# Loading w_down weights a pair ahead, and moving row and z loads, in an FNet/GeGLU kernel

## The chip, the cores and the metric

The kernel runs on one core of a Trainium2 chip. The metric is the device time of one execution in microseconds (us); the time before is the median of three runs. Beside them one execution was recorded by the hardware profiler, and everything that is read from the profile comes from that one.

The engines, as the profile names them: PE (TensorE, matmuls; PEld are its weight loads), DVE (VectorE), ACT (ScalarE), POOL (GpSimd) and SP (SyncE, which here only issues DMAs). DMAs are issued by SP and by POOL.

## What is computed

Four layers over x of 2048 rows and 512 columns, in single precision: a Fourier mixing layer and a gated feed-forward layer, twice.

```python
def _A_ref(x, dft_seq_re, dft_seq_im, dft_hid_re, dft_hid_im):
    a = jnp.einsum("bsd,ed->bse", x, dft_hid_re)
    b = jnp.einsum("bsd,ed->bse", x, dft_hid_im)
    y = jnp.einsum("ts,bse->bte", dft_seq_re, a) - jnp.einsum("ts,bse->bte", dft_seq_im, b)
    return y

def _B_ref(x, w_gate, w_up, w_down):      # w_gate, w_up: 512 x 1792, w_down: 1792 x 512
    return (_gelu(x @ w_gate) * (x @ w_up)) @ w_down

x = x + _A_ref(_layernorm(x, axis=-1), dft_seq_re, dft_seq_im, dft_hid_re, dft_hid_im)
x = x + _B_ref(_layernorm(x, axis=-1), w_gate, w_up, w_down)
x = x + _A_ref(_layernorm(x, axis=-1), dft_seq_re, dft_seq_im, dft_hid_re, dft_hid_im)
x = x + _B_ref(_layernorm(x, axis=-1), w_gate, w_up, w_down)
```

## The kernel before

**Products.** Every single precision operand is split in two parts, `hi` (ACT, line 150) and `lo` (DVE, line 152), and a product is three matmuls (`mm3`, lines 207 to 209). The kernel multiplies 2x2 blocks of matrices with seven products instead of eight, in Winograd's form: A11, A12, S1 to S4, A22 are the blocks and sums of blocks of one operand, B11 to B22 and T1 to T4 those of the other. The sums S1 to S4 of a weight are made once on DVE (`sums` in `weight_steps`, four operations of 256 columns), split (`divide`), kept in DRAM by POOL's DMAs and loaded from there afterwards: `wb` for w_gate and w_up, `wc` (the DRAM tiles `wdd`) for w_down.

**Layers.** `mix` does layers 0 and 2, `geglu(w, layer)` one half (w = 0 or 1: 1024 rows) of layers 1 and 3. In `geglu` the loop runs `up(n)` for 14 n; each n is one block column of w_gate or w_up and has seven products of six matmuls, and beside them one product of the down projection (`beside`, `down_product`), so 8 x 6 = 48 matmuls in most n. What is left of the down projection follows as the late part: 36 products of six (25 in the second half of layer 3, which ends with `plain_rows`). `down_order` gives their order.

**Queues and lists of small work.** The order of the work is written by hand. `queue` holds small pieces of work; each `step()` (one at each product of `up`, one at each product of the late part) takes one. `slow` is a second such list, of which every `PACE`-th step takes one. `chores` and `down_making` are two more. The framework then orders each engine's instructions by its own model of time; instructions of one engine run in that order. `issue_after` puts an instruction behind a given one on the same engine's queue.

**Operand stream.** `take()` hands out the next operand of PE and calls loads ahead of it (`load_next`, line 328, on SP): `wc` pieces two products ahead in `up`, six ahead in the late part. `stream["last"]` is the load that was called last.

**Slots.** SBUF has 98 slots of 128 x 512 (`sb`). They are handed out from a list in which a slot that comes free goes to the end; a load into a slot waits for the slot's last user.

The parts that the change touches:

- `down_piece`, `load_next` and `divide`: how a pair of w_down's blocks lies in DRAM. A tile `wdd[k]` holds three pairs of pieces of 1024 columns and one single. In a pair, the `hi` parts of both pieces come first and then the `lo` parts, so one piece is two rows of 256 columns (1 KB) in each partition.
- `down_making`: the making of w_down's seven pieces pairs k. For each k there are six entries, the load (three DMAs, lines 956 to 958, source `wdc`), `sums` and four `divide`. `DOWN_RUNS` says how many entries are taken where: 24 in layer 0, and 2 at each `up(n)` with n > 2 in the first half of layer 1.
- `terms_ahead` (line 573): mean and deviation of the rows of x for layer 2. It is called from `slow` in the second half of layer 1, eight times; each loads a row block (line 235, SP), and has three ACT passes (lines 565 to 570) and two small POOL operations.
- `block_steps(layer, 1)`: the second half's normed input z, transposed through DRAM (`turned`, tile `t`). `others[:ND]` are four `fetch` (line 687, eight DMAs of 64 KB each on SP for w = 1), the rest are differences and splits on DVE and ACT.
- `load_turned` (line 1249, DMAs of line 1253 on SP): loads the rows of x to which the down projection is added, in wide tiles, `xwide` for part 0 and `wide` for part 1, four DMAs of 256 KB each, in runs of 128 columns. It is called for part 0 at the last product beside `up`, where all seven pairs are used a second time after the loop, and for part 1 when the late part is a third through. Sums are added into these tiles by DVE in `turned_rows`.

Of the kernel before, what the change touches and what calls it, by code (L numbers as in the profile page):

```python
# [17 lines left out]
ND = D // P  # L18
# [15 lines left out]
PACE = 9  # L34
# [5 lines left out]
LEAD = 3  # L40
NK = NS // 2
SEED_AT = 3
DOWN_RUNS = ((0,0,0,0),(4,4,4,0),(4,4,4,0),2)


@with_exitstack
def fnet_geglu(ctx: ExitStack, tc: tile.TileContext, x_in, ws, wh, wgu, wdn, wdc, out):
# [32 lines left out]
    nc = tc.nc  # L80
# [56 lines left out]
    def f32(ap):  # L137
        return ap.bitcast(F32)
# [72 lines left out]
    half = slice(0, 256), slice(256, 512)  # L211
# [84 lines left out]
    wdd = {k: dram.tile([P, 7 * 512], F32, name=f"wc{k}") for k in range(NF // 2)}  # L296
    pieces = (("A11", "A12"), ("S2", "S3"), ("S1", "A22"), ("S4",))

    def down_piece(k, name):

        i = next(i for i, names in enumerate(pieces) if name in names)
        if i == 3:
            return wdd[k][:, 3 * 1024:]
        h = half[pieces[i].index(name)]
        return wdd[k][:, i * 1024:(i + 1) * 1024].rearrange("p (h c) -> p h c", h=2)[:, :, h]

    def halves(t):
        return t[:, :512], t[:, 512:]
# [1 line left out]
    def kept(place, parts):  # L310
        for t, a in zip(parts, halves(place)):
            nc.gpsimd.dma_start(a, f32(t))  # L312
# [3 lines left out]
    stream = {"loaded": 0, "split": 0, "used": 0, "more": 0}  # L316
    raws, parts = {}, {}

    def load_next():
        n = stream["loaded"]  # L320
        dtype, addresses, _, _ = items[n]
        raws[n] = []
        for a in addresses:
            t = sb.get(dtype)
            to = t if dtype == F32 else f32(t)
            if len(a.shape) == 3:
                to = to.rearrange("p (h c) -> p h c", h=2)
            stream["last"] = nc.sync.dma_start(to, a)
            raws[n].append(t)
        stream["loaded"] += 1  # L330
# [117 lines left out]
    NP = NF // 2  # L448
# [62 lines left out]
                items.extend((F32, (wdn[f],), plain, None) for f in range(2 * SEVEN[layer + 1, w], NF))  # L511


    queue, slow, steps_done, down_making = [], [], [0], []

    def step():
        if queue:
            run = queue.pop(0)
            if run is not None:
                run()  # L520
        steps_done[0] += 1
        if slow and steps_done[0] % PACE == 0:
            slow.pop(0)()


# [47 lines left out]
    def terms_ahead(layer, i, n):  # L573

        if i == 0:
            fresh["terms"] = x_load(layer, 0)
        x, junk = fresh.pop("terms"), sb.get()
        if i + 1 < n:
            fresh["terms"] = x_load(layer, i + 1)
        known[layer, i] = norm_terms(layer, i, x, junk)  # L580
        sb.put(x, junk)
# [156 lines left out]
    def mix(layer):  # L738
# [65 lines left out]
        def a11(b):  # L804
            chain = [ps8.get() for _ in range(2)]
            for k in range(NK):
# [6 lines left out]
                else:  # L813
                    six(chain, "B11", k, k == 0, k == NK - 1, "11" if b == NB - 1 else None)
                if b == FORE[layer] - 1 and k == SEED_AT:
                    a12_seeded(0)
# [104 lines left out]
        for n, (b, what) in enumerate(plan(layer)):  # L921
            if n == len(plan(layer)) - 1:
                if layer:
                    weight_load(0)
                    weight_load(1)
                while queue:
                    step()
            in_order[0] = layer or (b, what) not in plan(layer)[:2 * FORE[layer]]
            if layer == 0 and (b, what) == (0, "S2"):
                for k in range(NP):  # L930
                    load, making = down_weight_steps(k)
                    down_making.extend([load] + making)
            if what in stages:
                stages[what](b)
            else:
                hid_groups(b, what)
# [5 lines left out]
    wblocks = {n: dram.tile([P, 7 * 512], F32, name=f"wb{n}") for n in range(NF)}  # L942
# [3 lines left out]
    def weight_steps(n, raw=wgu, place=wblocks):  # L946

        src, v = [], {}

        def load():  # L950
            src.extend(sb.get() for _ in range(4))
            for i, names in enumerate((*pieces[:3], ("S4", "A21"))):
                for name, h in zip(names, half):
                    v[name] = src[i][:, h]
            with tc.issue_after(stream["last"].ins):
                nc.sync.dma_start(src[0], raw[n, :, :512])
                nc.sync.dma_start(v["A22"], raw[n, :, 512:768])
                nc.sync.dma_start(v["A21"], raw[n, :, 768:])

        def sums():  # L960
            before, in_order[0] = in_order[0], True
            plus(v["S1"], v["A21"], v["A22"])
            minus(v["S2"], v["S1"], v["A11"])
            minus(v["S3"], v["A11"], v["A21"])
            minus(v["S4"], v["A12"], v["S2"])
            in_order[0] = before

        def divide(i):
            def run():
                before, in_order[0] = in_order[0], True  # L970
                to = place[n][:, i * 1024:min((i + 1) * 1024, 7 * 512)]
                if i < 3:
                    t = split_slot(src[i])
                    kept(to, t)
                else:
                    t = (split_side(v["S4"]),)
                    nc.gpsimd.dma_start(to, f32(t[0]))
                if place is wblocks:
                    piece_here(n, i, t)
                else:  # L980
                    sb.put(*t)
                sb.put(src[i])
                in_order[0] = before
            return run

        return load, [sums] + [divide(i) for i in range(len(pieces))]

    def down_weight_steps(k):
        return weight_steps(k, wdc, wdd)
# [27 lines left out]
    def geglu(w, layer):  # L1017

        gs, h, acc = {}, {}, {0: [], 1: []}
# [31 lines left out]
        making = {}  # L1051
# [191 lines left out]
        def rows_moved(at, part, run):  # L1243

            for p in range(NT):
                v = xturned[part][p * 32:(p + 1) * 32]
                run(v.rearrange("t (j e) -> t j e", e=P), turned_view(at, part)[p])

        def load_turned(part):
            assert part or not sb.out("x")  # L1250
            pool = tpool if part else upool
            xturned[part] = pool.tile([P, NT * D], F32, name="wide" if part else "xwide")
            rows_moved(layer, part, lambda v, outside: nc.sync.dma_start(v, outside))

        def turned_rows(part, c, src):

# [58 lines left out]
        before_mix = w == 1 and layer < 3  # L1315
        plain_down = (layer, w) not in SEVEN
        if before_mix:
            slow.extend((lambda k=k: terms_ahead(layer + 1, k, NK)) for k in range(NK))
        if w == 0:
            norms, others = block_steps(layer, 1)  # L1320
            slow.extend(norms)
            ahead_of_all = others[:ND]
        if not plain_down and layer == 1 or layer == 3:
            sb.reclaim("x")
        first(0)
# [14 lines left out]
        elif pairs == NP:  # L1340
            load_turned(0)
        if w == 0:
            queue.extend(([None] * 4 if ahead_of_all else []) + others[len(ahead_of_all):])
        elif before_mix:
            queue.extend((lambda k=k: first_rows(layer + 1, k)) for k in range(NK))
        ahead = [(lambda n=n, i=i: piece_load(n, i)) for n in range(2) for i in range(len(pieces))]
# [154 lines left out]
```

## Time and profile before

| | us |
|---|---|
| median of 3 runs | 1626.48 |
| lowest and highest of them | 1619.25, 1629.77 |
| the profiled execution | 1617.86 |
| its span, first to last instruction | 1615.7 |
| mean granted PE clock in the span | 0.998 |

A line of the page's list of groups, here the first of the three matmuls of a product, and the two lines of the splits:

```profile
L207 PE MATMUL p<-s,s 128*128 128x512 f32 x2320 | 870.9, 391 | 10.7 <-DMA s<-wc 4.2
L150 ACT ACTIVATE s<-s 128x512 fp32r<-128x512 f32 (+1 forms) x809 | 454.9, 607 | 264.0 <-DVE s L183 72.9
L152 DVE TENSOR_TENSOR s<-s,s 128x512 fp32r<-128x512 f32 (+1 forms) x809 | 510.8, 669 | 121.0 <-ACT s L150 102.4
```

To be read as: line, engine, operation, output and inputs by the program's names (numbers of buffers left out; `s` are the slots, `p` the banks of PSUM), shape, count; then the group's busy time in us and the mean of one in ns; then the engine's idle time just before instructions of this group, and what ended most of it. The matmuls overlap in the pipeline, so that the mean of one is longer than the distance between two.

In timelines a row has its start and its length in us, the engine, line and operation, and in brackets how long the engine stood idle before it and what ended that. In the list of DMA issues, the last column is the median time from issue to landing.

### The profile page before, as it was taken

The numbers are of one execution on the slowest core, as the hardware profiler recorded it, in microseconds if no ns is written. First come the engines' busy times: TensorE is split into PE (matmuls) and PEld (weight loads), VectorE is DVE, ScalarE is ACT, GpSimd is POOL, SyncE is SP. The second block draws the span as 40 slices with busy tenths as digits, with TensorE's granted clock in tenths as the row PEclk, the third lists the DMA queues.
The fourth block names the chain that finished last, engine by engine and source line by source line (L and its number), as shares of the span: only waits on it lengthen the run. The fifth ranks groups of instructions, "written<-read, shape, count | busy, mean of one in ns | idle before, by whom it ended". The sixth has DMA issues, their size and how long they took to land. (4 is left out here: it accounts for less than half of the span.)

```text
span 1615.7 us, 22644 instructions
## 1 busy us (share of the span) xinstructions
PE 1598.9 (99%) x7008; PEld 1317.2 (82%) x7008; DVE 1133.3 (70%) x1958; ACT 885.4 (55%) x1711; POOL 260.9 (16%) x469
## 2 busy tenths in 40 slices
PE   9999999999999999999999999999999999999998
PEld 7888888888788878788788888888888888888887
DVE  8997778797689784445879967777764457743574
ACT  8955466664667552645648545565555455433460
POOL 4112121242456101100031000101400000000001
PEclk9999999999999999999999999999999999999999
DMA  9878887996988899954986866878989676895445
GB/s 359 292 266 305 284 312 263 339 327 214 335 307 320 271 309 304 248 168 138 319 285 201 269 238 224 283 246 283 267 282 301 191 222 189 309 302 175 125 150 156
DMA packets 258840, 419.14 MB, mean 259 GB/s; under 512 B 28512, under 2 KB 106592, under 8 KB 257696
## 3 DMA queue, kind: packets, MB, share of 16 engines
q1 hardware_dynamic: 234480, 336.16, 65.2%
q0 software_dynamic: 24240, 81.55, 14.2%
q8 instruction: 55, 0.90, 0.2%
q14 instruction: 65, 0.53, 0.1%
HBM read 341.31 MB, written 76.28 MB: 258 GB/s over the span
## 5 line engine op out<-in xcount | busy, mean ns | idle before, releaser
L208 PE MATMUL p<-s,s 128*128 128x512 f32 x2320 | 902.6, 390 | 0.0
L209 PE MATMUL p<-s,s 128*128 128x512 f32 x2320 | 895.8, 390 | 0.0
L207 PE MATMUL p<-s,s 128*128 128x512 f32 x2320 | 870.9, 391 | 10.7 <-DMA s<-wc 4.2
L150 ACT ACTIVATE s<-s 128x512 fp32r<-128x512 f32 (+1 forms) x809 | 454.9, 607 | 264.0 <-DVE s L183 72.9
L152 DVE TENSOR_TENSOR s<-s,s 128x512 fp32r<-128x512 f32 (+1 forms) x809 | 510.8, 669 | 121.0 <-ACT s L150 102.4
L207 PEld LDWEIGHTS p<-s,s 128*128 128x128 f32 x2320 | 436.2, 188 | 104.8 <-DMA s<-wc 5.5
L208 PEld LDWEIGHTS p<-s,s 128*128 128x128 f32 x2320 | 436.6, 188 | 91.0 <-DVE s L152 0.7
L209 PEld LDWEIGHTS p<-s,s 128*128 128x128 f32 x2320 | 436.5, 188 | 90.4
L187 DVE TENSOR_TENSOR s<-s,p 128x512 f32<-128x512 f32 x188 | 127.5, 685 | 175.6 <-PE p L209 146.5
L183 DVE TENSOR_TENSOR s<-s,s 128x512 f32<-128x512 f32 (+1 forms) x374 | 224.8, 619 | 7.9 <-PE p L208 3.7
L194 ACT ACTIVATE s<-p 128x512 f32<-128x512 f32 x232 | 134.0, 594 | 112.0 <-PE p L209 107.6
L1014 ACT ACTIVATE s<-s 128x512 f32<-128x512 f32 x84 | 52.7, 629 | 69.1 <-DVE s L187 66.9
L568 POOL TENSOR_SCALAR rstd<-rstd 128x1 f32<-128x1 f32 x40 | 22.3, 556 | 347.4 <-ACT s L567 331.9
L152 DVE TENSOR_TENSOR s<-xwide,s 128x512 fp32r<-128x512 f32 x71 | 48.3, 687 | 33.9 <-ACT s L150 33.6
L1028 DVE TENSOR_TENSOR s<-s,p 128x512 f32<-128x512 f32 x56 | 38.4, 686 | 31.5 <-PE p L209 28.2
L312 POOL DMA_DIRECT2D wb<-s x84 | 45.8, 548 | 90.1 <-ACT s L150 61.5
L190 DVE TENSOR_TENSOR s<-s,s 128x512 f32<-128x512 f32 (+1 forms) x68 | 41.1, 613 | 16.5 <-DMA s<-wdc 9.8
L150 ACT ACTIVATE s<-xwide 128x512 fp32r<-128x512 f32 x71 | 43.1, 621 | 17.2 <-DVE xwide L183 6.6
L591 ACT ACTIVATE s<-s,shift,rstd 128x512 f32<-128x512 f32 x56 | 45.0, 811 | 11.3 <-DMA s<-x 5.7
L201 ACT ACTIVATE p<-p 128x512 f32<-128x512 f32 x56 | 32.7, 585 | 27.9 <-PE p L209 27.7
L1014 ACT ACTIVATE s<-p 128x512 f32<-128x512 f32 x28 | 16.7, 598 | 52.8 <-PE p L209 49.1
L565 ACT ACTIVATE s<-s 128x512 f32<-128x512 f32 x33 | 20.7, 627 | 42.1 <-DMA s<-x 22.2
(100 smaller groups left out, 601.5 us busy)
## 6 DMA issues: line engine op xcount, KB each, us to landing
s<-ws SPq DMA_DIRECT2D x384, 256.0 KB, 4.9
s<-wb SPq DMA_DIRECT2D x294, 256.0 KB, 4.9
s<-wc SPq DMA_DIRECT2D x182, 256.0 KB, 4.7
s<-wh SPq DMA_DIRECT2D x116, 256.0 KB, 5.1
wb<-s POOLq DMA_DIRECT2D x98, 256.0 KB, 4.7
s<-x SPq DMA_DIRECT2D x59, 256.0 KB, 5.2
xwide<-ws SPq DMA_DIRECT2D x50, 256.0 KB, 4.8
wc<-s POOLq DMA_DIRECT2D x49, 256.0 KB, 6.0
```

The source lines that it names most:

```text
L150: newest["ACT"] = nc.scalar.activation(hi, src, AF.Copy)
L152: newest["DVE"] = nc.vector.tensor_tensor(lo, src, f32(hi), op=ALU.subtract)
L183: nc.vector.tensor_tensor(out, a, b, op=ALU.subtract)
L187: bank_read["DVE"] = nc.vector.tensor_tensor(out, a, b, op=ALU.add)
L190: nc.vector.tensor_tensor(out, a, b, op=ALU.add)
L194: bank_read["ACT"] = nc.scalar.activation(v, src, AF.Copy)
L207: nc.tensor.matmul(ps, ah, bh, start=start, stop=False, skip_group_check=True)
L208: nc.tensor.matmul(ps, ah, bl, start=False, stop=False, skip_group_check=True)
L209: nc.tensor.matmul(ps, al, bh, start=False, stop=stop, skip_group_check=True)
L312: nc.gpsimd.dma_start(a, f32(t))
L591: nc.scalar.activation(z, x, AF.Identity, bias=shift, scale=rstd)
L1014: nc.scalar.activation(t, g, AF.Gelu_apprx_tanh)
```

## The change

Four things change.

1. w_down in DRAM: within a pair of pieces the `hi` and `lo` of one piece now lie together, so a piece is read as one row of 512 columns (2 KB) in each partition, and a `divide` of w_down writes two rows of 256 columns (1 KB) for each of its two tiles.
2. `down_making`: up to k = `MIXED` = 4 the load of pair k stands before its own sums as now; with k = 4 also the load of pair 5 is called before the sums of pair 4, and then always the next pair's load before this pair's sums.
3. In the second half of layer 1, `slow` gets four empty entries ahead of the eight `terms_ahead`, and its pace is 7 steps instead of 9 (back to 9 at the next first half). In the first half of layer 1 the four fetches of z no longer run at `up(13)` but in the late part, behind four empty entries, and four more empty entries follow them. Layer 3 keeps its order.
4. `load_turned` in second halves (w = 1): its DMAs are put behind the operand load that was called last before it.

```diff
+MIXED = 4
...
-        h = half[pieces[i].index(name)]
-        return wdd[k][:, i * 1024:(i + 1) * 1024].rearrange("p (h c) -> p h c", h=2)[:, :, h]
+        at = i * 1024 + pieces[i].index(name) * 512
+        return wdd[k][:, at:at + 512]
...
-            if len(a.shape) == 3:
-                to = to.rearrange("p (h c) -> p h c", h=2)
...
-    queue, slow, steps_done, down_making = [], [], [0], []
+    queue, slow, steps_done, pace, down_making = [], [], [0], [PACE], []
...
-        if slow and steps_done[0] % PACE == 0:
+        if slow and steps_done[0] % pace[0] == 0:
             slow.pop(0)()
...
+                runs = [down_weight_steps(k) for k in range(NP)]
                 for k in range(NP):
-                    load, making = down_weight_steps(k)
-                    down_making.extend([load] + making)
+                    loads = [runs[k][0]] * (k <= MIXED) + [load for load, _ in runs[k + 1:k + 2] if k >= MIXED]
+                    down_making.extend([*loads, *runs[k][1]])
...
                     t = split_slot(src[i])
-                    kept(to, t)
+                    if place is wblocks:
+                        kept(to, t)
+                    else:
+                        for a, h in zip(t, range(2)):
+                            at = to.rearrange("p (n h c) -> p h n c", n=2, h=2)[:, h]
+                            nc.gpsimd.dma_start(at, f32(a).rearrange("p (n c) -> p n c", n=2))
...
-            rows_moved(layer, part, lambda v, outside: nc.sync.dma_start(v, outside))
+            with tc.issue_after(stream["last"].ins) if w else ExitStack():
+                rows_moved(layer, part, lambda v, outside: nc.sync.dma_start(v, outside))
...
         if before_mix:
-            slow.extend((lambda k=k: terms_ahead(layer + 1, k, NK)) for k in range(NK))
+            slow.extend([lambda: None] * 4 + [(lambda k=k: terms_ahead(layer + 1, k, NK)) for k in range(NK)])
+            pace[0] = 7
         if w == 0:
+            pace[0] = PACE
             norms, others = block_steps(layer, 1)
             slow.extend(norms)
-            ahead_of_all = others[:ND]
+            ahead_of_all = others[:ND] if layer in (3,) else []
...
         if w == 0:
-            queue.extend(([None] * 4 if ahead_of_all else []) + others[len(ahead_of_all):])
+            queue.extend([None] * 4 + others[len(ahead_of_all):ND] + ([] if ahead_of_all else [None] * 4) + others[ND:])
```

## The prediction

> **What bounds the kernel now.** I read the page first, for the engines' shares.
>
> ```profile
> span 1615.7 us, 22644 instructions
> PE 1598.9 (99%) x7008; PEld 1317.2 (82%) x7008; DVE 1133.3 (70%) x1958; ACT 885.4 (55%) x1711; POOL 260.9 (16%) x469
> ```
>
> TensorE (PE) has work 99% of the span, so only its few stops can be won. To price them I cut the span at the starts of the program's stages. Matmuls start in program order, so a stage's first one is found by counting: one `up(n)` is 8 products of 6 matmuls, a late part 36 products of 6. The view of busy time by windows then gives each stage's length (the first column behind the edges; the x counts take in one or two matmuls at the edges):
>
> ```profile
> core 0: us, PE busy (x) PEld busy (x) DVE busy (x) ACT busy (x) POOL busy (x), PEclk, DMA share, GB/s
> 424.27:435.15 10.88, 10.88 (x50) 9.02 (x48) 6.13 (x11) 7.99 (x17) 5.10 (x10) 1.00 1.07 341
> 435.15:451.48 16.33, 12.75 (x49) 10.12 (x48) 10.10 (x22) 6.22 (x12) 5.70 (x11) 0.90 0.88 323
> 557.62:609.36 51.74, 49.53 (x217) 40.44 (x216) 44.89 (x74) 27.43 (x49) 0.00 (x0) 1.00 0.90 300
> 643.36:658.64 15.28, 12.86 (x50) 9.70 (x48) 4.37 (x7) 12.95 (x39) 4.13 (x10) 0.89 1.11 286
> 764.72:815.62 50.90, 49.39 (x218) 40.41 (x217) 43.96 (x76) 32.75 (x61) 0.00 (x0) 1.00 0.86 286
> 1358.36:1408.24 49.88, 49.26 (x217) 40.50 (x216) 43.45 (x72) 26.86 (x48) 0.00 (x0) 1.00 0.91 308
> 1589.12:1615.72 26.60, 21.92 (x97) 17.85 (x95) 9.20 (x14) 0.00 (x0) 5.88 (x11) 1.00 0.78 237
> ```
>
> The first row is `up(2)` of layer 1, first half, undisturbed: 48 matmuls in 10.88 us, 0.2267 us each. A late part of 216 would take 48.96. What each stage loses is its length less that:
> - layer 1, first half (w=0), `up(3)`: 16.33 - 10.88 = 5.45; its late part: 51.74 - 48.96 = 2.78
> - layer 1, second half (w=1), `up(3)`: 15.28 - 10.88 = 4.40; its late part: 50.90 - 48.96 = 1.94
> - layer 3, first half, late part: 49.88 - 48.96 = 0.92
>
> Together 15.5 us. The last row, the 96 matmuls of `plain_rows`, loses 26.60 - 21.76 = 4.84 to the closing adds and stores, which the change leaves alone. PE's timeline shows one stop in each of the five stages and, in brackets, who ended it:
>
> ```profile
> 441.61 0.80 PE L207 MATMUL p<-s,s 128*128 128x512 f32 x1 [3.58 <-DVE s L1028]
> 572.96 0.50 PE L207 MATMUL p<-s,s 128*128 128x512 f32 x1 [2.09 <-DMA s<-wc]
> 649.79 1.22 PE L207 MATMUL p<-s,s 128*128 128x512 f32 x2 [2.18 <-ACT s L150]
> 779.65 0.50 PE L207 MATMUL p<-s,s 128*128 128x512 f32 x1 [1.51 <-DMA s<-wc]
> 1373.20 0.50 PE L207 MATMUL p<-s,s 128*128 128x512 f32 x1 [0.62 <-DMA s<-wc]
> ```
>
> In the first and third the stop is shorter than the loss, because the clock fell: PEclk 0.90 and 0.89, so 10% of 16.33 = 1.6 us and 11% of 15.28 = 1.7 us of each loss is half-speed clock. The Trainium skill (TensorE: Matmul & The Clock Gate, "Part 1: The HAM clock gate") has the clock halved after an idle window of about 3.4 us; by that the 2.18 us stop would have cost no clock and 2.7 instead of 4.4. The trace disagrees (0.89), and the measurement decides.
>
> **w_down a pair ahead (`MIXED`).** In `up(3)` the load and the sums of w_down pair 4 are now called together, and DVE stands at the sums:
>
> ```profile
> 429.98 0.33 SPq L957 DMA_DIRECT2D s<-wdc  x1
> 439.53 0.43 DVE L190 TENSOR_TENSOR s<-s,s 128x256 f32<-128x256 f32 x1 [6.79 <-DMA s<-wdc]
> ```
>
> DVE idles 6.79 us for that piece; the multiply of line 1028 that PE waits for stands behind it. After the change `up(3)` calls only the loads of pairs 4 and 5, and the sums come one `up`, 10.88 us, later, past the 439.5 at which the piece was there. The early load brings 0.5 MB, at 341 GB/s 1.5 us, ahead of w_gate/w_up loads on the same queue (SP), which have sums too. Its four slots are held longer. Gain between 5.45 and 5.45 - 1.5 - 1.6 (a 1.5 us stop with its clock) = 2.3; I take 5.0, since nearly the whole idle time belongs to this one wait. Pairs 0 to 3 keep their order.
>
> **Terms later, wide loads later (second halves).** ACT stops in `up(3)` of w=1 for the rows that `terms_ahead` reads:
>
> ```profile
> 637.25 2.58 SPq L235 DMA_DIRECT2D s<-x  x4
> 643.50 0.63 ACT L565 ACTIVATE s<-s 128x512 f32<-128x512 f32 x1 [6.16 <-DMA s<-x]
> 620.37 0.45 SPq L1253 DMA_DIRECT2D wide<-x  x1
> 642.15 2.95 SPq L1253 DMA_DIRECT2D xwide<-x  x4
> 655.74 2.34 SPq L1253 DMA_DIRECT2D xwide<-x  x4
> 646.00:652.00 6.00, 3.82 (x13) 2.76 (x12) 0.69 (x1) 6.00 (x21) 2.58 (x8) 0.82 1.16 203
> 573.60:577.00 3.40, 3.40 (x17) 2.80 (x16) 3.40 (x7) 1.67 (x3) 0.00 (x0) 1.00 1.06 379
> 740.00:760.00 20.00, 20.00 (x90) 16.57 (x89) 12.40 (x19) 9.85 (x18) 0.00 (x0) 1.00 0.35 109
> ```
>
> SP issues 12 wide loads here (4 into `wide`, twice 4 into `xwide`), 256 KB each, more than 100 us before the late part reads them. With them in flight the DMA engines are full and move 203 GB/s; with operand loads alone 379. So a wide load costs 262144 / 203 GB/s = 1.29 us against 0.69, and 12 cost 15.5 us of a full queue, in the stretch where the terms' rows and `wb` pieces are wanted. Two edits act here. Four empty entries and a pace of 7 put the first of the 8 terms (a row load on SP, three ACT passes, two POOL operations each) at step 29 to 35 instead of 1 to 9; with 7 steps per 10.88 us that is 45 to 54 us into the half, 655 to 664, and the last at step 84, about 740, ahead of the late part (764.7) that needs them. And `issue_after` puts `xwide` behind the operand load traced last before `up(13)`, where DMA is busy 0.35 (740 to 760): 8 loads, 10.3 us, fit. Cover: if they don't land before the late part's sixth product (764.7 + 6 x 1.36 = 772.9), DVE's add of line 187 stands in front of all splits. Gain between 0 (ACT waits elsewhere) and 4.40; I take 4.2, because both what waited and what filled the queue leave.
>
> `wide`, the second four, now come when the late part is a third through, into a full queue:
>
> ```profile
> 764.00:795.00 31.00, 29.49 (x130) 23.90 (x129) 26.19 (x46) 22.49 (x44) 0.00 (x0) 1.00 0.99 326
> 773.14 1.88 SPq L328 DMA_DIRECT2D s<-wc  x3
> ```
>
> DMA share is 0.99, and the 1.51 us stop at 779.65 is for one of the `wc` loads issued at 773 to 775. Four wide loads ahead of it add up to 4 x 1.29 = 5.2 us; behind it nothing, and the stop may go by slots being dealt otherwise. Between -1.9 and +5.2 + 1.7 (clock) = +6.9; I take +1.5, nearer the lower end, as most operand loads there run well ahead. Layer 3's second half has the same edit and no stop in the list; nothing. POOL's part of the terms (0.00 busy at 740) waits for nobody.
>
> **z fetched later (layer 1, w=0).** The four fetches are 32 DMAs on SP:
>
> ```profile
> 536.08 8.63 SPq L687 DMA_DIRECT2D s<-t  x8
> 547.70 10.18 SPq L687 DMA_DIRECT2D s<-t  x20
> 557.98 3.17 SPq L328 DMA_DIRECT2D s<-wc  x6
> 560.00:580.00 20.00, 17.79 (x78) 14.12 (x77) 20.00 (x34) 11.31 (x21) 0.00 (x0) 1.00 1.02 348
> ```
>
> Twenty take 10.18 us, so 32 take 16.3 us of issue. They stand in front of the `wc` loads that burst from 557.98; and DVE is busy all of 560 to 580, with the stop at 573 in it. Afterwards the fetches follow products 5 to 8 of the late part, and z's divisions start after 12 products instead of 4. That moves some 12 DVE operations (four first splits, six differences, two splits of `second`), at the 20.00 / 34 = 0.59 us of the row some 7 us, out of the full stretch; DVE has room behind it. Against it: fetches now pass between operand loads. Gain up to 2.78, loss as in rival C; I take 2.0. The queue of 30 entries, with 8 piece loads between, still ends in the late part by the loop that empties it.
>
> **Packets.** A `wc` piece is read as 2 KB rows (156 of 182 loads) and written as 1 KB rows (42 of 49 writes), the other way round than now.
>
> ```profile
> 569.00:573.00 4.00, 1.79 (x8) 0.86 (x6) 4.00 (x8) 3.55 (x7) 0.00 (x0) 1.00 1.06 364
> L312 POOL DMA_DIRECT2D wc<-s x42 | 22.7, 543 | 77.0 <-ACT s L150 68.3 <-DVE s L152 7.7 <-issue 0.7
> L1266 POOL DMA_DIRECT2D x<-wide x8 | 5.3, 663 | 185.3 <-DVE wide L190 185.3
> s<-wc SPq DMA_DIRECT2D x182, 256.0 KB, 4.7
> ```
>
> Mostly `wc` in flight: 364 GB/s, against 379 above: 0.72 to 0.69 us a load, 0.5 us over a burst of 18. I take 0.2 at layer 3's stop. The writes cost POOL at most the 663 ns of the scattered row instead of 543, 42 x 0.12 = 5 us, on an engine busy 16%: nothing. The last row (the list of DMA issues) gives the median from issue to landing, 4.7 us.
>
> Sum: -5.0 - 4.2 + 1.5 - 2.0 - 0.2 = -9.9 us. The profiled execution took 1617.86 (span 1615.7 and 2.2 around it); it becomes 1608. The median of the three runs is 1626.48, 8.6 above; taken off that, 1616.6.
>
> **Rivals.** *B, the late part pays.* The wide loads land in front of the operand loads: +6.9 in place of +1.5, net -4.5: 1622. For it: share 0.99 there. Against: 773 to 775 may come ahead of them. The Trainium skill (DMA: Bandwidth & Descriptors, "Rules for kernel authors") would have DMAs issued early and waited for late; deferring `wide` does the opposite, and the trace so far shows a harm of issuing early (the 203 GB/s stretch).
>
> *C, slower: fetches block SP.* 16.3 us of issue go between loads of products that last 1.36 us. Operand loads are called 6 products (8.2 us) ahead. If SP stands at the fetches no earlier than PE at product 5, PE stops 16.3 - 8.2 + 4.7 to land = 12.8, and 1.7 of clock: 14.5, and the 2.0 is not won. Net -7.9 + 14.5 = +6.6: 1633. It decides where SP's lead falls below 12.8 us; the trace has both, 13.4 at the first fetch (536.08 against `up(13)` at 549.46 = 557.62 - 36 x 0.2267) and next to none after the last.
>
> *D, all five stops go*: -15.5: 1611; a profile without their places refilled. *E, the order does nothing for the terms* (rows still late): -9.9 + 4.2 = -5.7: 1621.
>
> **Numbers.** Chances: forecast 0.53, B 0.15, C 0.10, D 0.13, E 0.09. The likeliest gives 1616. Range: unknown costs and the runs' own spread (1619.25 to 1629.77, 5 either way) give 1605 below, with D; above it reaches C, 1633. About 1% is what a measurement of this kernel can tell from no change: 16 us, about all that the five stops hold. Faster by more needs D and the spread: 0.16. Slower by more needs C and another stop like it: 0.10. Within: 0.74.
>
> **What would show it.** Right: no DVE wait for `wdc` at `up(3)`, 10.88 us there; no ACT wait for x rows in w=1's `up(3)`, L1253 issued after 735; 32 fetches past 550 without a PE stop. Wrong: a PE stop over 2 us for DMA near 780 (B) or in w=0's late part (C), or DVE standing at L187 for `xwide`.

## The result, and the profile after

| | before | after |
|---|---|---|
| median of the runs of one chip, us | 1622.57 (8 runs, 1619.25 to 1629.77) | 1616.88 (8 runs, 1615.34 to 1618.03) |
| the profiled execution, us | 1617.86 | 1617.71 |
| its span, us | 1615.7 | 1615.9 |
| mean granted PE clock | 0.998 | 0.997 |

The ratio of after to before is 0.9958, 95% interval 0.994 to 0.9975: 4 to 10 us less, 6.8 in the middle. By the prediction's own bound of 1% that is no change, and the forecast of 1616.0 lies 0.9 from the median.

The two profiled executions are equally long, though the medians differ by 5.7 us. The profiled execution of before was short, 4.7 below the median of its kernel; after's was 0.8 above its own. So the profiles tell where stops came and went, and the medians tell what a version is worth. A second profile of each kernel (below) is there for the same reason.

The page of after, its head and the line of DMA packets:

```profile
span 1615.9 us, 22618 instructions
PE 1601.3 (99%) x7008; PEld 1317.5 (82%) x7008; DVE 1132.7 (70%) x1958; ACT 885.3 (55%) x1711; POOL 271.4 (17%) x469
DMA packets 238872, 419.14 MB, mean 259 GB/s; under 512 B 28512, under 2 KB 66656, under 8 KB 237728
```

PE is busy 99% as before. To see what moved, the view of busy time by windows, cut at the same stages as in the prediction, with its columns (the first after the edges is the stage's length, the last three the clock, the DMA share and GB/s):

```profile
437.00:447.88 10.88, 10.88 (x50) 9.01 (x49) 5.98 (x13) 8.22 (x18) 5.88 (x11) 1.00 0.99 345
553.96:602.91 48.95, 48.95 (x217) 40.54 (x216) 44.92 (x74) 27.10 (x47) 2.62 (x4) 1.00 0.94 325
636.91:647.79 10.88, 10.88 (x49) 9.01 (x48) 4.36 (x7) 4.41 (x10) 0.74 (x2) 1.00 0.60 187
753.87:807.22 53.35, 51.24 (x217) 41.39 (x216) 44.24 (x76) 34.96 (x66) 0.00 (x0) 0.97 0.97 306
883.38:896.22 12.84, 11.61 (x50) 8.67 (x48) 11.70 (x20) 4.25 (x9) 1.07 (x2) 1.00 0.72 220
1224.15:1242.15 18.00, 14.07 (x50) 11.01 (x48) 6.48 (x10) 8.68 (x18) 1.35 (x3) 0.81 1.00 281
1359.11:1408.48 49.37, 49.29 (x217) 40.48 (x216) 41.78 (x69) 26.34 (x46) 0.00 (x0) 1.00 0.88 312
```

Three of the five lossy stages are now exactly as long as their matmuls: `up(3)` of layer 1, first half (10.88) and second half (10.88), and the first half's late part (48.95). The late part of the second half lost more than before (53.35 - 48.96 = 4.39, before 1.94). And two stages lose that lost nothing before: one in layer 2 (12.84 - 10.88 = 1.96) and, the largest of all, `up(2)` of layer 3, first half: 18.00 instead of 10.88, a loss of 7.12 with the clock at 0.81.

What each stage lost (its length less 0.2267 us for each of its matmuls, as in the prediction), in us, in the profile of each kernel that the next section tells of:

| kernel | L1 w=0 `up(3)` | its late part | L1 w=1 `up(3)` | its late part | L2, all | L3 w=0 `up(2)` | its late part | span |
|---|---|---|---|---|---|---|---|---|
| before | 5.45 | 2.78 | 4.40 | 1.94 | 0.1 | 0 | 0.92 | 1615.7 |
| before, again | 4.19 | 1.65 | 6.59 | 1.68 | 0.1 | 0 | 0.55 | 1618.8 |
| after | 0 | 0 | 0 | 4.39 | 2.1 | 7.12 | 0.41 | 1615.9 |
| after, again | 0 | 0 | 0 | 2.90 | 4.0 | 6.99 | 0 | 1617.1 |
| steps of layer 3 as before | 0 | 0 | 0 | 3.95 | 2.1 | 0 | 0 | 1607.2 |
| wide loads ordered in layer 3 too | 0 | 0 | 0 | 3.43 | 3.9 | 0 | 1.93 | 1609.8 |
| pairs as before | 6.64 | 0 | 0 | 6.37 | 2.1 | 6.36 | 0.19 | 1622.4 |
| z as before | 0 | 1.19 | 0 | 1.18 | 4.2 | 0 | 0.14 | 1610.2 |
| terms as before | 0 | 0 | 0 | 1.70 | 7.3 | 7.42 | 0 | 1619.0 |
| wide loads as before | 0 | 0 | 0.32 | 0.85 | 1.1 | 7.02 | 0 | 1610.3 |
| layout as before | 0 | 0 | 0 | 7.51 | 2.1 | 9.20 | 0.41 | 1624.6 |
| layout alone, on before | 7.58 | 0 | 3.51 | 0.75 | 0.1 | 0 | 0 | 1613.5 |
| steps and wide loads as before | 0 | 0 | 0 | 0.65 | 0.1 | 0 | 0 | 1601.3 |
| the same, `xwide` loaded once | 0 | 0 | 0 | 0.56 | 0.1 | 0 | 0.69 | 1602.9 |

(The loss in layer 2 of after is nearly all at 883.38, the last block of its first stage. Layer 0 is left out, with the start-up in it: it loses 4.7 in before but 8.2 in the second look at before, and 6.6 in both looks at after, so spans of two profiles can differ by 3 us for that alone. A few stages with about 1 us at the ends are left out too.)

PE's timeline of after shows the two stops of most weight, the first with two short ones ahead of it (columns as in the prediction's timelines):

```profile
766.61 0.73 PE L208 MATMUL p<-s,s 128*128 128x512 f32 x2 [0.34 <-ACT s L151]
767.65 0.73 PE L208 MATMUL p<-s,s 128*128 128x512 f32 x2 [0.31 <-ACT s L151]
769.85 0.80 PE L208 MATMUL p<-s,s 128*128 128x512 f32 x1 [1.46 <-DMA s<-wc]
770.44 0.63 PE L209 MATMUL p<-s,s 128*128 128x512 f32 x1
...
1230.96 0.80 PE L208 MATMUL p<-s,s 128*128 128x512 f32 x1 [3.93 <-ACT s L1019]
1231.55 0.63 PE L209 MATMUL p<-s,s 128*128 128x512 f32 x1
...
1237.36 0.39 PE L208 MATMUL p<-s,s 128*128 128x512 f32 x1
```

The stop at 1230.96 is 3.93 us, and from there to 1237.36 the 15 matmuls take 6.40 us, 0.43 each, where they would take 3.40 at 0.2267: 3.0 of the 7.1 us are half-speed clock.

### The profile page after: what moved, and what is told of

It is laid out like the page before. It is cut to its first block, busy times and chain, and to the rows that moved or that the text cites. A ratio compares the mean times of both kernels' runs of the same rounds, so it can differ in the third digit from the quotient of the medians.

```text
span 1615.9 us, 22618 instructions
## 1 busy us (share of the span) xinstructions
PE 1601.3 (99%) x7008; PEld 1317.5 (82%) x7008; DVE 1132.7 (70%) x1958; ACT 885.3 (55%) x1711; POOL 271.4 (17%) x469
## 2 busy tenths in 40 slices
DMA packets 238872, 419.14 MB, mean 259 GB/s; under 512 B 28512, under 2 KB 66656, under 8 KB 237728
```

## The experiments

Each run's kernel differs from after (or, where said, from before) by the edit shown, and was timed beside before on the same chip; ratios are to that. The runs were made on several chips, so two versions are compared by their ratios, and by their medians only where they ran on one chip.

### The two kernels once more

> The kernel before, unchanged, for a second profile. Theory (each stop has its own cause in the order of the work): the same five stages of the feed-forward layers lose again 5.4, 2.8, 4.4, 1.9 and 0.9 us within 1 us each, and a time nearer the median of its eight runs (1622.6) comes from these growing or from the half-speed clock after them. Rival (stops fall by chance of the run's transfers): the losses sit in other stages or differ by more than 2 us.

> The changed kernel, unchanged. Theory: up(3) of both halves of layer 1 and the first half's late part lose under 0.3 us again, the second half's late part 3 to 5, and up(2) of layer 3's first half 7 (a stop of 3.9 and two half-speed stretches). Time 0.994 to 0.998 of before. Rival (chance): the 7 us stop is absent or elsewhere.

Measured: the second look at before took 1620.93 us with a span of 1618.8. After took 1617.89 (12 runs), ratio 0.9976 [0.9961, 0.9991], against 1622.73 for before (23 runs); its profile lost 6.99 in `up(2)` of layer 3. So the gain is small but real, and the stop in layer 3 belongs to the kernel, not to one execution. The early stops of before come again as well, in the same five stages, but not within the 1 us that was expected: three of the five differ by more, and `up(3)` of the second half by 2.2, past the rival's 2. What differs most is layer 0, by 3.5. That is the resolution of a single profile here.

### The new stop: two steps of the list in layer 3

In the profile of after, SP's DMA issues and ACT's wait ahead of the stop at 1230.96 (the timeline):

```profile
1213.13 2.93 SPq L1259 DMA_DIRECT2D xwide<-x  x4
1219.83 3.82 SPq L245 DMA_DIRECT2D s<-x  x4
...
1228.42 0.63 ACT L564 ACTIVATE s<-s 128x512 f32<-128x512 f32 x1 [5.96 <-DMA s<-x]
```

ACT stands for 5.96 us at the sum over a row block of x (a norm out of `slow`); the row's four DMAs were issued at 1219.83, behind four wide loads. Behind ACT's wait stand the evictions and the gelu of line 1019 for which PE waits. The same place in before:

```profile
1217.91 2.73 SPq L1253 DMA_DIRECT2D xwide<-x  x4
1225.77 3.68 SPq L244 DMA_DIRECT2D s<-x  x4
1233.21 0.64 ACT L565 ACTIVATE s<-s 128x512 f32<-128x512 f32 x1 [1.89 <-PE p L209]
```

There the norm stands 2.69 us behind the start of `up(2)` (1233.21 - 1230.52) and finds its row. In after ACT stands ready for it at 1222.46 (1228.42 - 5.96), 1.69 us ahead of the start of `up(2)` at 1224.15. So the norm is 4.4 us earlier in ACT's order. The code says why: `step()` counts every step since the start, and `slow` gives an entry when the count is a multiple of 9. Layer 3 starts at step 756 = 84 x 9 in before. In after the longer queue of layer 1's first half takes two more steps to empty, and layer 3 starts at 758; every entry of its list comes two steps earlier.

The first test gives the two steps back, and nothing else:

```diff
         if w == 0:
             pace[0] = PACE
+            if layer == 3:
+                steps_done[0] -= 2
```

> The changed kernel with the step count set back by 2 at the first half of layer 3, so that the slow list there is taken at the same steps as in the kernel before. Theory (the two steps more that the longer list of layer 1 takes move the norms of layer 3 onto the wide loads): up(2) there loses under 1 us instead of 7.1, time 5 to 7 us below the changed kernel, 0.991 to 0.994 of before. Rival (slots or chance): it loses its 7 us still, time as the changed kernel.

Measured: 1612.96 us (6 runs), ratio 0.9938 [0.9916, 0.9959], span 1607.2. In its timeline the row is still issued behind the wide loads, but ACT comes to it later:

```profile
1209.91 4.04 SPq L1259 DMA_DIRECT2D xwide<-x  x4
1220.14 4.64 SPq L245 DMA_DIRECT2D s<-x  x4
1225.59 0.63 ACT L564 ACTIVATE s<-s 128x512 f32<-128x512 f32 x1 [1.90 <-DMA s<-x]
```

1225.59 is again 2.69 us behind the start of `up(2)` (1222.90), the wait is 1.90, and the stage loses nothing. The second test leaves the steps as in after and takes the wide loads out of the way instead, in layer 3's first half too behind the operand load called last:

```diff
-            with tc.issue_after(stream["last"].ins) if w else ExitStack():
+            with tc.issue_after(stream["last"].ins) if w or layer == 3 and not part else ExitStack():
```

> The changed kernel, and in the first half of layer 3 the wide loads of part 0 also put behind the operand load called last; step count as changed. Theory (the norms' rows are late because eight wide loads stand in front of them): up(2) there loses under 1 us instead of 7 although the norms come at the same steps; time 5 to 7 us below the changed kernel. Rival (the two steps alone decide, whatever else is in the queue): up(2) loses 3 us or more.

Measured: 1612.19 us (6 runs), ratio 0.9945 [0.9932, 0.9958], span 1609.8. The norm is as early as in after, and its row is there:

```profile
1215.30 1.72 SPq L245 DMA_DIRECT2D s<-x  x4
1222.40 0.63 ACT L564 ACTIVATE s<-s 128x512 f32<-128x512 f32 x1
```

So it takes both, the norm two steps earlier and its row behind the wide loads. Either one put right removes the stop. The steps are worth 4.9 us in the medians of one chip (1617.89 to 1612.96); by the ratios (0.9938 and 0.9945) either is worth 5 to 6 against after's second measurement (0.9976) and 2 to 3 against its first (0.9958). With the wide loads moved, the late part of the same half loses 1.93 in place of 0.41 or nothing, at a stop that DVE ends.

### The edits undone one at a time

**Pairs.** All loads again called together with their own sums:

```diff
-MIXED = 4
+MIXED = 7
```

> The changed kernel with w_down's pairs loaded in their own turn again (MIXED 7). Theory: up(3) of layer 1's first half loses 4 to 6 us again, with DVE idle over 5 us for wdc, and the other stages stay as in the changed kernel; time 4 to 6 us above it. Rival (the later fetches and the packets had removed that stop): up(3) loses under 1 us and the time stays.

Measured: 1625.15 us (12 runs), ratio 1.0012 [0.9999, 1.0026], 7.3 above after on the same chip, where 4 to 6 were expected; in this profile the late part of the second half loses 6.37 as well. DVE's wait and PE's stop are back, in the timeline:

```profile
441.27 0.43 DVE L191 TENSOR_TENSOR s<-s,s 128x256 f32<-128x256 f32 x1 [7.42 <-DMA s<-wdc]
...
443.36 0.79 PE L208 MATMUL p<-s,s 128*128 128x512 f32 x1 [4.20 <-DVE s L1033]
```

In after the same sums find their piece. SP issues the six loads of pairs 4 and 5 between 427.01 and 436.14, and DVE's line, 10 us behind the last, has no wait at all:

```profile
436.14 0.33 SPq L958 DMA_DIRECT2D s<-wdc  x1
...
446.14 0.42 DVE L191 TENSOR_TENSOR s<-s,s 128x256 f32<-128x256 f32 x1
```

**z.** The four fetches again at `up(13)` in layer 1, and the queue as long as before:

```diff
-            ahead_of_all = others[:ND] if layer in (3,) else []
+            ahead_of_all = others[:ND]
```

> The changed kernel with the four fetches of z back at up(13) of layer 1's first half (the rest as changed). Theory: that half's late part loses 1.6 to 2.8 us again; the list is as short as before, so the step count of layer 3 is that of the kernel before and up(2) there loses under 1 us instead of 7; net 4 to 6 us below the changed kernel, about 0.993 to 0.995 of before. Rival (the fetch blocks nothing; the late part's stop went by the slots): the late part loses nothing, and layer 3 decides alone, 7 us below the changed kernel.

Measured: 1614.75 us (9 runs), ratio 0.9959 [0.9942, 0.9975]: not slower than after, although the late part of the first half loses 1.19 again, because the layer 3 stop goes with the two steps (7.12 to 0 in the table). The forecast of 0.993 to 0.995 is missed by little. In the profiles the edit wins 1.19 and costs 7.12 some 660 us later. In after the fetches, seen on SP's timeline, lie between 538.96 and 563.81:

```profile
538.96 1.78 SPq L686 DMA_DIRECT2D s<-t  x4
...
562.02 1.79 SPq L686 DMA_DIRECT2D s<-t  x4
```

They start 15 us ahead of the late part (553.96), and PE has no stop in it. The stop that comes back is not the one that had gone: before's 2.09 us was for an operand load, and the longest here is 0.33 us, for a split:

```profile
567.12 0.47 PE L208 MATMUL p<-s,s 128*128 128x512 f32 x1 [0.33 <-DVE s L153]
```

**Terms.** The eight row blocks for layer 2 again at once and with a pace of 9:

```diff
-            slow.extend([lambda: None] * 4 + [(lambda k=k: terms_ahead(layer + 1, k, NK)) for k in range(NK)])
-            pace[0] = 7
+            slow.extend((lambda k=k: terms_ahead(layer + 1, k, NK)) for k in range(NK))
```

> The changed kernel with terms_ahead at its old steps (pace 9, no empty entries); the wide loads stay late. Theory A (the queue full of wide loads made the rows late): up(3) of the second half of layer 1 loses under 1 us, the wide loads being gone. Theory B (the rows were asked for too early, whatever else was in the queue): it loses 3 us or more again.

Measured: 1616.58 us (10 runs), ratio 0.9971 [0.9954, 0.9988], as after. `up(3)` of the second half loses nothing, so the four empty entries and the pace of 7 are not needed for it once the wide loads are ordered. The late part loses less than in after (1.70) and layer 2 more (7.3); the profiled execution is the longest of the ten, 4.2 us above their median.

**Wide loads.** No order for them in second halves:

```diff
-            with tc.issue_after(stream["last"].ins) if w else ExitStack():
+            if True:
                 rows_moved(layer, part, lambda v, outside: nc.sync.dma_start(v, outside))
```

> The changed kernel with the wide loads of second halves free to go early again; the terms stay late. Theory A (wide loads fill the queue): ACT or PE still stops in up(3) to up(5) of layer 1's second half, 1 to 4 us, now for other loads. Theory B (only the early terms): none there. In its late part, rival B of the prediction (the wide loads land in front of operand loads) expects the loss to fall from 2.9 to 4.4 to under 2; if the wide loads come behind the operand load that is late, it stays within 1 us of the changed kernel's.

Measured: 1612.95 us (7 runs), ratio 0.9955 [0.9936, 0.9973], span 1610.3. By the time alone it can't be told from after, whose ratios are 0.9958 and 0.9976 with intervals that overlap this one; the stages tell more. `up(3)` of the second half (from 636.47) loses 0.32. ACT still waits for a row, 4.12 us, but just ahead of that stage, at a place where PE hardly notices:

```profile
634.58 0.63 ACT L564 ACTIVATE s<-s 128x512 f32<-128x512 f32 x1 [4.12 <-DMA s<-x]
```

So of the two edits meant for that stage each is enough by itself, and the one that orders the wide loads is not only unneeded but costs: the late part of the same half loses 0.85 without it and 4.39 with it (2.90 in the second look). The timelines of SP, ACT and PE around the late part, after first (it starts at 753.87):

```profile
731.60 2.02 SPq L1259 DMA_DIRECT2D xwide<-x  x4
741.08 2.85 SPq L1259 DMA_DIRECT2D xwide<-x  x4
746.81 0.80 SPq L236 DMA_DIRECT2D s<-x  x2
753.10 1.52 ACT L590 ACTIVATE s<-s,shift,rstd 128x512 f32<-128x512 f32 x2 [2.92 <-DMA s<-x]
753.94 1.27 SPq L327 DMA_DIRECT2D s<-wc  x3
763.18 1.75 SPq L327 DMA_DIRECT2D s<-wc  x3
765.26 2.93 SPq L1259 DMA_DIRECT2D wide<-x  x4
```

Then without the order (the late part starts at 753.75):

```profile
746.69 0.81 SPq L236 DMA_DIRECT2D s<-x  x2
750.65 1.52 ACT L590 ACTIVATE s<-s,shift,rstd 128x512 f32<-128x512 f32 x2 [0.59 <-DMA s<-x]
751.49 1.87 SPq L327 DMA_DIRECT2D s<-wc  x3
761.30 1.90 SPq L327 DMA_DIRECT2D s<-wc  x3
767.58 0.51 PE L208 MATMUL p<-s,s 128*128 128x512 f32 x1 [0.52 <-DMA s<-wc]
```

In both kernels PE's stop ends with the second load of a group of three, issued at 763.96 in after and at 762.07 without the order: 10.1 and 8.3 us into the late part. In after that group is 1.8 us later, and PE stops 1.46 instead of 0.52. It is not `wide`, the tile loaded a third through, that stands ahead of this load: `wide` is issued at 765.26, behind it. What comes earlier is `xwide`, twice, at 731.60 and 741.08. SP issues the two rows of x that ACT needs next at the same time in both kernels (746.81 and 746.69), but behind the second loading of `xwide`, and the three operand loads that SP puts between, they come later: ACT waits 2.92 us for them in place of 0.59 and starts at 753.10 in place of 750.65. SP itself waits for them with its next operand loads. The view of SP's own waits between 747 and 756 has, in after and then without the order,

```profile
SPq L327 <- DMA s<-x: 5.5, 1, 5.5
```

```profile
SPq L327 <- DMA s<-x: 3.1, 1, 3.1
```

so the run of operand loads that ends in the late group begins at 753.94 in place of 751.49, in both kernels 0.84 us behind ACT's row. The chain from `xwide` over the row to the late load is read from these lines; the second loading was not left out, nor `xwide` ordered without `wide`, in a kernel that keeps the order.

**Layout.** The three hunks of `down_piece`, `load_next` and `divide` as before:

```diff
-        at = i * 1024 + pieces[i].index(name) * 512
-        return wdd[k][:, at:at + 512]
+        h = half[pieces[i].index(name)]
+        return wdd[k][:, i * 1024:(i + 1) * 1024].rearrange("p (h c) -> p h c", h=2)[:, :, h]
...
```

> The changed kernel with w_down's pieces in DRAM as before (1 KB rows read, 2 KB rows written). Theory: time within 2 us of the changed kernel; the late parts lose up to 1 us more, since a load takes 0.72 instead of 0.69 us in a full queue. Rival: the packets carry a good part of the gain, and the late parts of first halves lose 2 us more each.

Measured: 1622.37 us (10 runs), ratio 1.0008 [0.9991, 1.0024]: without the layout the whole rest of the change is worth nothing that can be measured. The loss is not where the rival had it, in the late parts of first halves (0 and 0.41, as in after): the late part of the second half loses 7.51 and `up(2)` of layer 3 loses 9.20, in a profiled execution that is 4 us above its median. As that was far more than forecast, another run put the same three hunks on before and nothing else.

> The kernel before, and of the change only how w_down's pieces lie in DRAM (2 KB rows read, 1 KB rows written). Theory A (the packets themselves are worth what undoing them cost, about 5 us): 0.996 to 0.998 of before, the late parts of layers 1 and 3 lose 1 us less each. Theory B (they matter only where the later wide loads crowd the late part): within 2 us of before, late parts as before.

Measured: 1613.39 us (11 runs), ratio 0.9949 [0.9932, 0.9965], that is 8 to 9 us less than before (8.3 by the ratio, 9.4 by the medians), and more than theory A had. In its profile `up(3)` stops as in before, and the late parts lose 0, 0.75 and 0 in place of 2.78, 1.94 and 0.92. The first of these is the stage that the later fetches of z were meant for; here 20 fetches still stand in one run on SP just ahead of that late part, as in before:

```profile
550.18 10.50 SPq L685 DMA_DIRECT2D s<-t  x20
```

So the late part of the first half loses nothing with the fetches moved and the old layout (0), and nothing with the new layout and the fetches unmoved (0): for the stop of 2.09 us either is enough. The windows view of the late part's full stretch in the second half, of before and of this kernel:

```profile
765.00:780.00 15.00, 13.49 (x60) 10.70 (x59) 13.64 (x25) 10.67 (x21) 0.00 (x0) 1.00 1.03 335
```

```profile
765.00:780.00 15.00, 14.54 (x65) 11.71 (x64) 14.60 (x27) 11.08 (x22) 0.00 (x0) 1.00 1.01 360
```

With the DMA engines as full (1.03 and 1.01), 360 GB/s move in place of 335, 7% more; from 562 to 570, in the first half's late part, it is 346 in place of 326. The landings of the single loads in the trace give the price without a second kernel. Between 773 and 790 in before, where one 256 KB load lands behind the other, those of 1 KB rows land 0.75 us after the one ahead of them (10 loads, median), and those of 2 KB rows 0.68 (11 loads); in this kernel all are of 2 KB rows and take 0.68. The page of this kernel has the same line of packets as after's (66656 under 2 KB); before's has

```profile
DMA packets 258840, 419.14 MB, mean 259 GB/s; under 512 B 28512, under 2 KB 106592, under 8 KB 257696
```

That fits the late parts, in part: nine loads of 1 KB rows land in before from 768.5 up to the one that ends the stop at 779.65, and nine times 0.07 us is 0.6, while the stop is 1.05 shorter here (1.51 to 0.46). It does not account for all of the 9 us: the profiles' spans differ by 2.2 (1615.7 to 1613.5), or 5.3 with the second look at before. The edit also changes the order in which the framework puts the instructions, so the gain can't be given to the packets alone. That stays open.

### Both costs taken out

With the two steps given back and the wide loads as before:

> The changed kernel without the ordering of wide loads and with layer 3's step count set back by 2. Theory: the gains add, 4 us of the ordering and 5 of the steps; about 1607 to 1610, 0.990 to 0.993 of before; up(3) of layer 1 loses under 0.5 us in both halves, its late parts under 1, up(2) of layer 3 under 1. Rival (each was measured against its own runs' spread): 1613, as either alone.

Measured: 1603.78 us (4 runs, 1602.39 to 1604.88), ratio 0.9889 [0.9875, 0.9903], 18 us less than before on that chip (1621.46), more than forecast, and the shortest here. Its page:

```profile
span 1601.3 us, 22617 instructions
PE 1594.1 (100%) x7008; PEld 1314.5 (82%) x7008; DVE 1132.7 (71%) x1958; ACT 887.6 (55%) x1711; POOL 269.8 (17%) x469
```

It differs from the run with the two steps alone (0.9938 [0.9916, 0.9959]) only by the order of the wide loads, and the intervals don't meet: that order costs about 8 us there (0.0049 x 1622), if the ratios of two chips may be set against each other. In the spans it is 5.9 (1607.2 to 1601.3): 3.3 of it in the late part of layer 1's second half (3.95 to 0.65), 2.1 in layer 2.

One more run also took out the second loading of `xwide` where seven pairs are used:

```diff
-        elif pairs == NP:
-            load_turned(0)
```

> As best_a, and xwide is loaded once instead of twice in the three halves that use all seven pairs (the second load of the same rows is left out). Theory: 12 wide loads of 1.3 us fewer in queues that stop nobody any more, so within 2 us of best_a. Rival: the queue is still what PE's remaining stops wait for, and it is 3 us or more below best_a.

Measured: 1604.64 us (4 runs), ratio 0.9894 [0.9878, 0.9911], the same as the run above. The loading that is done twice costs nothing once nobody waits behind it.

## Why the prediction was right, and where only the number was

The forecast of the time came out, the direction and the class too. But it is a sum of errors that cancel: that the number came so near is luck, and the single steps are worth more than it. Its signs of being right came, with two times missed by little: the first loads of `xwide` went out at 731.60 and not after 735, and 11 of the 32 fetches before 550.

**The starting point.** 1616 was the forecast gain of 9.9 taken from a median of three runs, 1626.48. With eight runs before is at 1622.57, 4 lower. The gain of after was 4 to 10 us, 6.8 in the middle; the number was met because too large a gain was taken from too high a start.

**w_down a pair ahead, -5.0.** Right, and shown: 5.45 to 0 in the profile, 6.64 back when undone, 7.3 in the medians. The early load cost no stop; the lower bound of 2.3 was not needed.

**Terms and wide loads later, -4.2.** The size is right (4.40 to 0), the reason half right. The prediction gave it to both edits, "because both what waited and what filled the queue leave"; the runs show either one alone to be enough (0 and 0.32). A stage that is credited to two edits together must be tried with each alone. Rival E, that the order does nothing for the terms, falls.

**Wide loads in the late part, +1.5.** In that stage alone the loss grew by 2.4 (1.94 to 4.39; by 1.2 between the second looks), near the term. But the order as a whole cost 5.9 us of span, 8 in the ratios, when the other cost was out. The step that failed is "8 loads, 10.3 us, fit": `xwide` was counted as free since the DMA engines were busy 0.35 there. The bytes fit, but the rows behind the second loading came 2.4 us later for ACT, and SP's run of operand loads waited for them. Rival B had the size of the whole (+6.9) more nearly, by another path: it had `wide` in front of the operand loads, and `wide` came behind the one that stopped PE. The Trainium skill (DMA: Bandwidth & Descriptors, "Rules for kernel authors") would have DMAs issued early and waited for late; the prediction set a harm of issuing early against it, the 203 GB/s stretch. The runs agree with the rule: with the terms out of the way the early issue harms by 0.32 in that stage, and the version with early loads is the shortest.

**z fetched later, -2.0.** The size is right (2.78 to 0), the reason in doubt. Undone, 1.19 came back, at a stop for a split and not for an operand load, and the layout alone takes the 2.78 away too, with the fetches where they were. The prediction gave that stage to z and nothing of it to the packets. Rival C, SP blocked by the fetches, did not come: the framework let SP start them 15 us ahead of the late part, where the prediction had put them behind products 5 to 8.

**The step that was missing.** "The queue of 30 entries, with 8 piece loads between, still ends in the late part by the loop that empties it" is true, and was taken as the end of the matter. But that loop takes steps, the steps are counted, and the count sets when each entry of the other list comes, a half and a layer later. The prediction had no term for `up(2)` of layer 3, and it cost 7.1 us in the profile and 5 in the medians. Without it the change is at 0.9938, 10.1 us less than before, near the forecast sum of 9.9, but with the wide loads costing more and the layout gaining more than their terms.

**Packets, -0.2.** Mis-sized by far. Undone, the layout costs 5 to 8 us (1.0008 against 0.9976 and 0.9958); alone it gains 8 to 9. The price of one load was set at half of what the landings show (0.72 to 0.69 us from the rows of 364 and 379 GB/s; 0.75 to 0.68 measured), and it was counted only at the smallest stop. It can act in every stretch in which the DMA engines are full and PE waits for a load in them. As an estimate, 7% of some 20 us in each late part is 1.4 us, about the size of the stops that went.

**What stays open.** The share of the packets in the layout's 9 us; which of `xwide` and `wide` costs the late part its time; why layer 2 loses 2 to 7 us in every version with the wide loads ordered, 1.1 with that order alone undone, and 0.1 in before, with the layout alone and in the two shortest versions (its stops are for splits by ACT and DVE); why the same kernel loses 4.7 or 8.2 us in layer 0.

## What to carry to other kernels

When a change moves work in a hand-written order, count everything that the order's own counter drives: a list that is two entries longer shifts every later entry that is taken by a modulus, and the cost can show a whole layer further on, at a place that the diff does not name. Undo the edits of a bundle one at a time, and put the small ones on the old kernel alone: of this one, the layout was worth as much as the pairs though it looked like a trifle, the order of the wide loads cost more than it gave, two stops had two edits of which either was enough, and the sum hid all of that. And set the sum of stage losses of a profile against several executions, since the profiled one can lie 5 us from the median of its kernel.

## What was not expected of the hardware

**The clock.** The stop of 1.46 us at 769.85 in after, with two of about 0.3 us in the 4 us ahead of it, was followed by matmuls 0.43 us apart and a clock of 0.97 over the stage. The stop of 1.51 at 779.65 in before was not (0.50 for the matmul behind it, clock 1.00). So the length of a stop alone does not decide it in these two. The Trainium skill (TensorE: Matmul & The Clock Gate, "Part 1: The HAM clock gate") has the clock halved by an idle window of about 3.4 us and calls that window free-running; this trace shows it halved with far less idle time than that. The stop of 3.93 us was followed by 6.4 us of half speed.

**Row size.** Reading the w_down pieces in 2 KB rows in place of 1 KB rows raised what full DMA engines moved from 335 to 360 GB/s. The engines' busy share did not show it (1.03 and 1.01); only the GB/s did, and the landings: 0.75 us for 256 KB in 1 KB rows and 0.68 in 2 KB rows, side by side in one stretch of before. The wide loads, 256 KB in runs of 512 bytes, land 1.3 to 1.5 us apart (the four issued from 741.08 in after).
